# First global queries and keys by GpSimd's casting DMA, first memsets on VectorE, in an attention and feed-forward kernel

## The chip, the cores and the metric

The kernel runs on one core of a Trainium2 chip. A core has TensorE (PE, matrix products), VectorE (DVE), ScalarE (ACT), GpSimd (POOL) and SyncE (SP), all running their own instruction streams and waiting for one another through semaphores. DMAs are issued from SP, ScalarE or GpSimd; only the ones issued from GpSimd change the type on the way here (float32 in memory to bfloat16 on chip). The metric is the device time of one execution in microseconds (us), smaller is better.

## What is computed

For 8 batches and 8 heads there are 512 local tokens and 32 global tokens of 64 numbers each. Global queries attend to everything; a local query attends to the 32 global keys and to the local keys at most 32 positions away. The result goes, heads side by side, through two large matrix products with a gelu-like function between them.

```python
def _attn_ref(q_l, k_l, v_l, q_g, k_g, v_g):
    ...
    k_all = np.concatenate([k_g, k_l], axis=2)
    v_all = np.concatenate([v_g, v_l], axis=2)
    s_g = scale * np.matmul(q_g, k_all.transpose(0, 1, 3, 2))
    out_g = np.matmul(sm(s_g), v_all)
    s_ll = scale * np.matmul(q_l, k_l.transpose(0, 1, 3, 2))
    mask = np.abs(pos[:, None] - pos[None, :]) <= window      # window 32
    s_ll = np.where(mask, s_ll, -1000000000.0)
    s_lg = scale * np.matmul(q_l, k_g.transpose(0, 1, 3, 2))
    a_l = sm(np.concatenate([s_lg, s_ll], axis=-1))
    out_l = np.matmul(a_l, np.concatenate([v_g, v_l], axis=2))
    return np.concatenate([out_g, out_l], axis=2)

def _moe_ref(x, w_in, w_out):                                 # x: 4352 x 512
    h = x @ w_in                                              # w_in: 512 x 2048
    g = h * (1.0 / (1.0 + np.exp(-1.702 * h)))
    return g @ w_out                                          # w_out: 2048 x 512
```

## The kernel before

The work goes batch by batch, each batch in two quads of four heads (a quad's four heads lie in the four groups of 32 partitions). The program writes the order of every engine's instructions out by hand; the framework only adds the waits. While batch i goes through the two large products (`h_mm`, L711, and `o_mm`, L739), the attention of batch i + 1 is woven in between, so that TensorE always has work. Only the first batch has nothing to hide behind: its loads, casts, transposes and exponentials are the head of the program.

In the head, quad 0 (object `a`) and quad 1 (object `c`) of batch 0 are prepared. Keys and queries of quad 0 come as float32, in two halves each, into the tile `early`: k by ScalarE's DMA queue (L146), q by SP's (L147). ScalarE casts k's first half and then both halves of q (`cast_act`, L774); VectorE casts k's second half (L783). VectorE then transposes blocks of 32 x 32: k into `kT` (`Tk`, L335) and q into the tile `q` (`Tq`, L339), each in halves. The global queries and keys of the first two quads come by `load_g32` (L134) into float32 tiles, `g32q` ahead of q's halves on SP's queue and `g32k` behind k's halves on ScalarE's; VectorE casts them to bfloat16 (`cast_g32`, L137), transposes them (`transpose_g`, L269), and copies the global queries into the borders of the tile `q` (`ext`, L349).

TensorE begins with small products of a zero tile (L190), adds the mask's bias to the scores (`B`, L361), then three filler products of zeros (`zero`, L771), then the scores (`S`, L382), in two parts for quad 0: the first needs q's first half, the second q's second half. ScalarE takes the exponentials (`X`, L415 and L410), and so on through both quads up to L481 and L499, after which the first large product (L711) starts.

GpSimd's stream starts with memsets (`ones32` L154, `rvg` L155, `bd` L157 and L160, a border of `v` L165), the step pattern (`affine_select`, L166) from which VectorE builds `ident`, `band` and `bias` (L213 to L215), and the memset of `near_mask` (L176, read by GpSimd's `mask_near` and only needed by batch 1). Then it issues DMAs that cast: q and k of quad 1 (L78, L79), the global values `rvg` (L122, L123), and by `load_rest` v (L275), the weights w_in (L287) and w_out (L279), and batch 1. From its ninth DMA on, GpSimd issues a DMA only when its eighth-last has landed: the trace shows w_in's second load waiting for rk's landing and its eighth for v's.

The order of VectorE's instructions in the head, as the program writes it:

```python
    cast_g32("q", rqg)
    transpose_g(0, 2, "q")
    a.ext((0, 1))
    a.Tk(0, 8)
    nc.vector.tensor_copy(rk[:, 0, halves[1]], k32[:, halves[1]])
    a.Tk(8, 16)
    a.Tq(0, 8)
    a.Tq(8, 16)
    a.ext((2, 3))
    cast_g32("k", rkg)
    transpose_g(0, 2, "k")
    ...
    c.Tq()
    c.ext()
    c.Tk()
```

Of the kernel before, what the change touches and what calls it, by code (L numbers as in the profile page):

```python
# [12 lines left out]
F32 = mybir.dt.float32  # L13
# [7 lines left out]
def kernel(  # L21
# [12 lines left out]
    nc = tc.nc  # L34

    B, H, Sl, D = q_l.shape
# [18 lines left out]
    consts = ctx.enter_context(tc.tile_pool(name="consts", bufs=1))  # L55
# [8 lines left out]
    qf = q_l.rearrange("b (u j) (r t) d -> b (j r) u (t d)", j=4, t=16)  # L64
    kf = k_l.rearrange("b (u j) (r t) d -> b (j r) u (t d)", j=4, t=16)
    qgf = q_g.rearrange("b (u j) s d -> (j s) (b u) d", j=4)
    kgf = k_g.rearrange("b (u j) s d -> (j s) (b u) d", j=4)
# [4 lines left out]
    def load(b, us=(0, 1), kq=True):  # L72
        if b not in loaded:
            loaded[b] = (ld.tile([128, 2, 16 * D], BF16, name="rk"),
                         ld.tile([128, 2, 16 * D], BF16, name="rq"))
        if kq:
            s = slice(us[0], us[-1] + 1)
            nc.gpsimd.dma_start(out=loaded[b][1][:, s], in_=qf[b][:, s])  # L78
            nc.gpsimd.dma_start(out=loaded[b][0][:, s], in_=kf[b][:, s])  # L79
# [3 lines left out]
    def v_view(b, n):  # L83
        return vtiles[b % 2][:, : 8 * n * (D + 2)].rearrange("p (u j c d) -> p u j c d", u=2, j=4, c=n)
# [31 lines left out]
    rqg = consts.tile([128, NQ, D], BF16)  # L116
    rkg = consts.tile([128, NQ, D], BF16)

    rvg = consts.tile([128, 2, D + 2], BF16)

    def load_turned(eng, out_, in_):
        eng.dma_start(out=out_[32:128], in_=in_[0:96])  # L122
        eng.dma_start(out=out_[0:32], in_=in_[96:128])  # L123

    def load_g(lo, hi, names="kq"):
        for name, dst, src in (("k", rkg, kgf), ("q", rqg, qgf)):
            if name in names:
                nc.gpsimd.dma_start(out=dst[:, lo:hi, :], in_=src[:, lo:hi, :])

    g32 = {}  # L130

    def load_g32(name, src, eng):
        t = g32[name] = consts.tile([128, 2, D], F32, name="g32%s" % name)
        eng.dma_start(out=t, in_=src[:, 0:2, :])  # L134

    def cast_g32(name, t):
        nc.vector.tensor_copy(t[:, 0:2, :D], g32[name])  # L137

    load(0, kq=False)
    rk, rq = loaded[0]  # L140
    early = ld.tile([128, 4, TB], F32, name="early", bufs=1)
    k32, q32 = (early[:, 2 * i : 2 * i + 2].rearrange("p a b -> p (a b)") for i in range(2))
    halves = (slice(0, 8 * D), slice(8 * D, 16 * D))
    load_g32("q", qgf, nc.sync)
    for f in halves:
        nc.scalar.dma_start(out=k32[:, f], in_=kf[0][:, 0, f])  # L146
        nc.sync.dma_start(out=q32[:, f], in_=qf[0][:, 0, f])  # L147
    load_g32("k", kgf, nc.scalar)


    step = consts.tile([128, 289], BF16)
    nc.vector.memset(step, 1.0)
    ones32 = consts.tile([128, 32], BF16)
    nc.gpsimd.memset(ones32, 1.0)  # L154
    nc.gpsimd.memset(rvg[:, :, D:], 1.0)  # L155
    bd = consts.tile([128, 4, 32], BF16)
    nc.gpsimd.memset(bd, 0.0)  # L157
    for j in range(4):
        r = (j + 1) % 4
        nc.gpsimd.memset(bd[32 * r : 32 * r + 32, j, :], 1.0)  # L160
    vturn = [consts.tile([128, n, 8, D + 2], BF16, name="vt%d" % n) for n in (5, 4)]
    for i in range(2):
        vtiles.append(consts.tile([128, 8 * 6 * (D + 2)], BF16, name="v%d" % i))
        if i == 0:
            nc.gpsimd.memset(v_view(i, 4)[:, :, :, :, D:], 1.0)  # L165
    nc.gpsimd.affine_select(  # L166
        out=step, in_=step, pattern=[[1, 289]], compare_op=ALU.is_ge,
        fill=0.0, base=-97, channel_multiplier=-1,
    )
    tick = consts.tile([1, 2], F32)  # L170

    def after(x):
        nc.gpsimd.tensor_copy(tick[:, 0:1], x[0:1, 0:1])  # L173

    near_mask = consts.tile([128, 27, 32], BF16)
    nc.gpsimd.memset(near_mask, 1.0)  # L176
    load(0, (1,))
    load_turned(nc.gpsimd, rvg[:, 0:2, :D], vgf[:, 0:2])

    w_in_sb = wts.tile([128, 4, NKC, d_ff // 4], BF16)  # L180
# [4 lines left out]
    warm = consts.tile([128, 512], BF16)  # L185
# [63 lines left out]
    def mask_near():  # L249
        def zero(lo, hi, first, last, by):  # L250
            nc.gpsimd.memset(near_mask[lo:hi, first:last:by], 0.0)

        zero(0, 96, 4, 24, 5)
        zero(0, 96, 24, 27, 1)
        for g, first, late in ((1, 0, True), (0, 1, False), (2, 1, True), (1, 2, False), (2, 3, False), (0, 4, True)):
            mask_put(g, first, 24, 5, late, near_mask)
        zero(64, 96, 0, 24, 5)
        zero(0, 32, 2, 24, 5)
        zero(0, 64, 3, 24, 5)
        mask_put(3, 24, 25, 1, True, near_mask)  # L260

    qgT = consts.tile([128, 2, 40], F32)
    nc.vector.memset(qgT[:, :, 32:], 0.0)
    kgT = consts.tile([128, 2, 32], F32)
    def transpose_g(lo, hi, names="qk"):
        for name, dst, s in (("q", qgT, rqg), ("k", kgT, rkg)):
            if name not in names:
                continue
            nc.vector.transpose(dst[:, lo:hi, :32], s[:, lo:hi].bitcast(F32))  # L269

    def load_v2(b):
        vp = v_l[b].rearrange("(u h) (c p) d -> u p h c d", u=2, p=128)
        for u in range(2):
            for p in (slice(0, 64), slice(64, 128)):
                nc.gpsimd.dma_start(out=v_view(b, 4)[p, u, :, :, :D], in_=vp[u, p])  # L275

    def load_rest():
        def w_out(g):
            nc.gpsimd.dma_start(  # L279
                out=w_out_sb[:, 4 * g : 4 * g + 4, :].rearrange("p (g e) m -> p g (e m)", e=2),  # L280
                in_=w_out_r[:, 2 * g : 2 * g + 2, :])

        load_v2(0)
        n = d_ff // 4
        for part in range(4):
            for u in range(2):
                nc.gpsimd.dma_start(out=w_in_sb[:, part, 2 * u : 2 * u + 2],  # L287
                                    in_=w_in_r[u][:, :, part * n : part * n + n])
        w_out(1)
        load(1, (0,))  # L290
        mask_near()
        load_g(2, 4)
        load(1, (1,))
        w_out(0)
        w_out(2)
        load_v(1)
        w_out(3)
# [4 lines left out]
    def pbank(name):  # L302
        return psP.tile([128, 512], F32, name=name, tag="p")
# [440 lines left out]
    def o_out(i, tci, op):  # L744
        ob = moe.tile([128, d_model], F32, name="ob", bufs=6)
        last = i == B and tci == B // 4 - 1
        for lo, hi in ((0, 320), (320, 512)) if last else ((0, 512),):
            if last:
                op = pbank("op")
                for fc in range(FC):  # L750
                    nc.tensor.matmul(op[:, lo:hi], lhsT=gTs[i][:, fc, tci * 128 : tci * 128 + 128],  # L751
                                     rhs=w_out_sb[:, fc, lo:hi], start=(fc == 0), stop=(fc == FC - 1))
            nc.scalar.activation(ob[:, lo:hi], op[:, lo:hi], AF.Copy, scale=0.5 if i > 1 else 1.0)  # L753
            if i == B:
                rows = out.rearrange("(b s) m -> s b m", s=S)[16 * tci : 16 * tci + 16]
                nc.sync.dma_start(out=rows[:, :, lo:hi], in_=ob[:, lo:hi])
                continue
            for j in range(4):
                if 1 <= i < B:
                    r = i * S + Sg + 128 * tci + 64 * (j // 2)  # L760
                    rows = out[r : r + 64, :].rearrange("(b g q) m -> g q b m", b=2, g=2)[j % 2]
                else:
                    rows = out[i * S + Sg : (i + 1) * S, :].rearrange("(r t) m -> t r m", t=16)[4 * tci + j]
                eng = nc.gpsimd if (i, tci, j) == (B - 2, 3, 3) else nc.sync
                eng.dma_start(out=rows[..., lo:hi], in_=ob[32 * j : 32 * j + 32, lo:hi])  # L765

    a, c = Quad(0), Quad(1)

    def zero(n, ps):
        for _ in range(n):  # L770
            nc.tensor.matmul(ps, lhsT=warm[:, 0:128], rhs=warm, start=False, stop=False, skip_group_check=True)  # L771

    def cast_act(r, f32, hf):
        nc.scalar.activation(r[:, 0, halves[hf]], f32[:, halves[hf]], AF.Copy)  # L774

    cast_act(rk, k32, 0)
    cast_act(rq, q32, 0)
    cast_act(rq, q32, 1)
    cast_g32("q", rqg)
    transpose_g(0, 2, "q")  # L780
    a.ext((0, 1))
    a.Tk(0, 8)
# [2 lines left out]
    a.Tq(0, 8)  # L785
    a.Tq(8, 16)
    a.ext((2, 3))
    cast_g32("k", rkg)
    transpose_g(0, 2, "k")
    load_rest()  # L790
    a.B(0)
    a.B(1, split=True)
    zero(3, a.bk[1][3])
    a.S(0, added=True, part=0)
    a.S(0, added=True, part=1, fill=8)
    a.X(0)
# [3 lines left out]
    c.Tq()  # L800
    c.ext()
    c.Tk()
    c.B(0)
    a.K()
    a.XK()
# [40 lines left out]
    a, c = nq[1]  # L846
# [43 lines left out]
    a, c = nq[2]  # L890
# [162 lines left out]
    for st in range(4):  # L1053
        o_mm(B, st)
    o_out(B, 1, None)


# [28 lines left out]
```

## Time and profile before

| | us |
|---|---|
| median of 3 runs | 293.13 (292.99 to 293.31) |
| the profiled execution | 293.34 |
| its span, first to last instruction | 291.6 |
| PE busy in the span | 285.1 (98%) |
| DVE, ACT, POOL busy | 190.7, 163.7, 81.4 |
| granted TensorE clock, mean | 1.000 |

The profile is one execution, taken by the hardware's profiler. A row of its timeline has the start, the duration, engine and line, the operation, the tile written and the tile read, their shapes, a count, and in brackets how long the engine had stood idle before it and what ended that. An engine's name with a q (SPq) is its issuing of DMAs. The chain of work is followed back from the last instruction: each row is what the next one waited for, with start, duration and line. In the DMA view, q10 is ScalarE's queue, q1 SP's and q0 GpSimd's; a row has packets, MB, and the time of the packets as a share of 16 engines' time in the window (packets overlap, so it can exceed 100%).

### The profile page before, as it was taken

The page shows a single profiled execution, that of the slowest core. Times are in us where ns is not written, and L with a number is a line of the kernel's source. Part 1 is how long each engine was busy: PE and PEld are TensorE (multiplying, and loading weights), DVE is VectorE, ACT ScalarE, POOL GpSimd, SP SyncE. Part 2 cuts the span into 40 slices and gives each one's busy share as a digit, 9 for nine tenths or more (in the row PEclk, how much of TensorE's full clock was granted, in tenths as well). Part 3 has the DMA queues.
Part 4 walks back from the last instruction along what each step waited for, and adds up shares of the span by engine and source line. Part 5 has one row for each costly group of instructions (what it writes and reads, how often), then busy time and mean ns, then how long its engine had stood idle before and what let it go on. Part 6 is the DMA issues. An engine that isn't in the chain of part 4 may idle for free.

```text
span 291.6 us, 9957 instructions
## 1 busy us (share of the span) xinstructions
PE 285.1 (98%) x4321; PEld 145.0 (50%) x4321; DVE 190.7 (65%) x388; ACT 163.7 (56%) x272; POOL 81.4 (28%) x149
## 2 busy tenths in 40 slices
PE   7899999999999999999999999999999999999994
PEld 6454445444554455445544455445544544456553
DVE  5581856444799878787778767877777554773310
ACT  4847855665557644674556563674556541763421
POOL 8877675752155000460007000530000000000000
PEclk9999999999999999999999999999999999999999
DMA  7999993999779913899269913993272022101123
GB/s 200 175 201 207 203 144 28 193 258 205 117 120 219 190 38 70 201 197 83 58 170 179 115 42 72 219 191 46 50 191 49 2 49 65 36 0 38 37 64 84
DMA packets 56780, 35.05 MB, mean 120 GB/s; under 512 B 43312, under 2 KB 45616, under 8 KB 56736
## 3 DMA queue, kind: packets, MB, share of 16 engines
q0 software_dynamic: 47168, 17.08, 51.5%
q1 hardware_dynamic: 9008, 16.75, 22.0%
q8 instruction: 34, 0.56, 0.8%
q10 hardware_dynamic: 560, 0.59, 0.6%
q14 instruction: 10, 0.08, 0.1%
HBM read 35.19 MB, written 8.91 MB: 151 GB/s over the span
## 4 chain that ended last, share of the span: by engine, by line
PE 94%; ACT 2%; DMA 2%; SPq 0%; DVE 0%; issue 0%
PE op L739 41%; PE hp L711 38%; PE s L588 5%; PE ov L622 4%; PE s L711 2%; DMA early<-in_q_l_dram 2%; PE op L751 1%; ACT ebuf L415 1%; PE s L664 1%; PE ov L481 1%; ACT ebuf L410 1%; PE s L622 0%; PE s L382 0%; PE ov L458 0%; ACT rq L774 0%; ACT ek L446 0%
## 5 line engine op out<-in xcount | busy, mean ns | idle before, releaser
L739 PE MATMUL op<-w_out_sb,gT 128*128 128x512 bf16 x528 | 124.1, 380 | 0.0
L711 PE MATMUL hp<-xL,w_in_sb 128*128 128x512 bf16 x480 | 104.9, 379 | 0.0
L722 DVE SCALAR_TENSOR_TENSOR gT<-th,hp 128x512 bf16<-128x512 f32 (+1 forms) x112 | 71.5, 649 | 29.7 <-ACT th L721 29.1
L711 PEld LDWEIGHTS <-w_in_sb 128*128 128x128 bf16 x576 | 56.1, 98 | 64.3
L721 ACT ACTIVATE th<-hp 128x512 f32<-128x512 f32 (+1 forms) x112 | 62.7, 566 | 36.1 <-PE hp L711 35.8
L739 PEld LDWEIGHTS <-gT 128*128 128x128 bf16 x528 | 48.2, 98 | 51.2
L598 ACT ACTIVATE ebuf<-s 128x704 bf16<-128x704 f32 x48 | 33.7, 754 | 27.3 <-PE s L588 27.3
L753 ACT ACTIVATE ob<-op 128x512 f32<-128x512 f32 (+2 forms) x35 | 20.5, 585 | 42.2 <-PE op L739 35.9
L604 DVE TENSOR_TENSOR ebuf<-ebuf,mask 128x1024 bf16<-128x1024 bf16 (+1 forms) x24 | 17.4, 723 | 19.7 <-ACT ebuf L598 19.7
L99 POOL DMA_DIRECT2D v<-in_v_l_dram x35 | 27.3, 795 | 5.8 <-DMA rk<-in_k_l_dram 3.7
L553 DVE STREAM_TRANSPOSE kl<-rk 128x512 f32<-128x512 f32 x14 | 14.7, 1050 | 18.0 <-DMA rk<-in_k_l_dram 18.0
L636 DVE TENSOR_TENSOR xn<-ov,rc 128x384 bf16<-128x384 f32 (+1 forms) x39 | 21.1, 542 | 1.3
L173 POOL CAST tick<-gT 1x1 f32<-1x1 bf16 x3 | 0.5, 173 | 70.6 <-DVE gT L722 70.6
L718 ACT ACTIVATE gT<-hp 128x512 bf16<-128x512 f32 x24 | 14.3, 598 | 5.6 <-PE hp L711 5.5
L588 PEld LDWEIGHTS <-kT 32*128 32x128 bf16 x1344 | 12.4, 92 | 10.2 <-issue 9.8
L765 POOL DMA_DIRECT2D out_dram<-ob x1 | 0.5, 521 | 54.7 <-ACT ob L753 54.7
L622 PEld LDWEIGHTS <-ebuf 128*32 128x32 bf16 (+1 forms) x1312 | 12.5, 94 | 6.0 <-issue 3.0
L588 PE MATMUL s<-q,kT 32*128 32x32 bf16 (+2 forms) x1344 | 15.2, 184 | 0.0
L567 DVE STREAM_TRANSPOSE q<-rq 128x512 f32<-128x512 f32 x14 | 14.7, 1046 | 0.0
L622 PE MATMUL ov<-v,ebuf 128*32 128x66 bf16 (+1 forms) x656 | 12.4, 196 | 0.0
L635 DVE RECIPROCAL rc<-ov 128x6 f32<-128x6 f32 (+1 forms) x39 | 7.1, 183 | 7.0 <-PE ov L622 6.7
L622 PE MATMUL ov<-vt,ebuf 128*32 128x66 bf16 x528 | 10.6, 195 | 0.0
(119 smaller groups left out, 208.6 us busy)
## 6 DMA issues: line engine op xcount, KB each, us to landing
out_dram<-ob SPq DMA_DIRECT2D x127, 64.0 KB, 2.7
v<-in_v_l_dram POOLq DMA_DIRECT2D x35, 96.0 KB, 8.2
vt<-v SPq DMA_DIRECT2D x12, 264.0 KB, 4.9
vt<-v SPq DMA_DIRECT2D x6, 495.0 KB, 4.7
w_in_sb<-in_moe_w_in_dram POOLq DMA_DIRECT2D x8, 256.0 KB, 7.8
w_out_sb<-in_moe_w_out_dram POOLq DMA_DIRECT2D x4, 512.0 KB, 10.1
rq<-in_q_l_dram POOLq DMA_DIRECT2D x4, 512.0 KB, 5.9
rk<-in_k_l_dram POOLq DMA_DIRECT2D x4, 512.0 KB, 8.6
```

The lines of the kernel that those rows point to most:

```text
L99: nc.gpsimd.dma_start(out=vt[0:96, c, :, :D], in_=vs[96 * c : 96 * c + 96])
L553: nc.vector.transpose(self.kl.rearrange("p (r t) -> p t r", t=16), loaded[self.b][0][:, self.u].bitcast(F32))
L588: nc.tensor.matmul(bank(self.ps, j)[:, 0:LW].rearrange("p (t q) -> p t q", q=32)[:, os], lhsT=self.k[p, k0 : k0 + 128, e], rhs=self.q[p, t ...
L598: nc.scalar.activation(self.E[rnd][:, 2 * i : 2 * i + 2, :], self.ps[i][:, :, :LW], AF.Exp, scale=scale)
L604: nc.vector.tensor_mul(e, e, m.to_broadcast([128, 4, n]))
L622: nc.tensor.matmul(ov[32 * j : 32 * j + 32, 66 * to : 66 * to + 66], lhsT=self.E[rnd][0:n, j, 32 * o : 32 * o + 32], rhs=self.vs[rho][0:n, ...
L636: nc.vector.tensor_mul(xn[:, lo // 2 : hi // 2].rearrange("p a h w b -> p a b h w"), o3[:, 0:n, 0:D].rearrange("p (a b) (w h) -> p a b h w ...
L711: nc.tensor.matmul(hp[:, : width(i)], lhsT=w_in_c[:, fc // 4, kc, fc % 4 // 2, :, fc % 2], rhs=(xL[i] if i < B else xG)[:, kc, :], start=( ...
L721: nc.scalar.activation(th[:, :n], hp[:, :n], AF.Tanh, scale=0.851)
L722: nc.vector.scalar_tensor_tensor(gTs[i][:, fc, :n], in0=th[:, :n], scalar=1.0, in1=hp[:, :n], op0=ALU.add, op1=ALU.mult)
L739: nc.tensor.matmul(op, lhsT=gTs[i][:, fc, tci * 128 : tci * 128 + 128], rhs=w_out_sb[:, fc, :], start=(first and fc == 4 * f4), stop=(fc = ...
L753: nc.scalar.activation(ob[:, lo:hi], op[:, lo:hi], AF.Copy, scale=0.5 if i > 1 else 1.0)
```

## The change

The first global queries and keys are no longer loaded as float32 by SP and ScalarE and cast by VectorE. GpSimd's queue loads them with the cast, the queries as the very first DMA, the keys between the loads of quad 1's q and k. SP's and ScalarE's queues carry only the halves of q and k of quad 0. The memsets of `ones32`, `bd` and `near_mask` move from GpSimd to VectorE: the first two behind that of `qgT`, the last behind quad 1's transposes; `load_rest` moves in the program text to behind that one. The first three filler products become half as wide, and two output stores of the first batch are issued as two halves of 16 rows.

```diff
-    def load_g32(name, src, eng):
-        t = g32[name] = consts.tile([128, 2, D], F32, name="g32%s" % name)
-        eng.dma_start(out=t, in_=src[:, 0:2, :])
-    def cast_g32(name, t):
-        nc.vector.tensor_copy(t[:, 0:2, :D], g32[name])
+    load_g(0, 2, "q")
     load(0, kq=False)
...
-    load_g32("q", qgf, nc.sync)
     for f in halves:
         nc.scalar.dma_start(out=k32[:, f], in_=kf[0][:, 0, f])
         nc.sync.dma_start(out=q32[:, f], in_=qf[0][:, 0, f])
-    load_g32("k", kgf, nc.scalar)
...
     ones32 = consts.tile([128, 32], BF16)
-    nc.gpsimd.memset(ones32, 1.0)
-    nc.gpsimd.memset(rvg[:, :, D:], 1.0)
     bd = consts.tile([128, 4, 32], BF16)
-    nc.gpsimd.memset(bd, 0.0)
-    for j in range(4):
-        r = (j + 1) % 4
-        nc.gpsimd.memset(bd[32 * r : 32 * r + 32, j, :], 1.0)
...
-        if i == 0:
-            nc.gpsimd.memset(v_view(i, 4)[:, :, :, :, D:], 1.0)
     nc.gpsimd.affine_select(
         out=step, in_=step, pattern=[[1, 289]], compare_op=ALU.is_ge,
         fill=0.0, base=-97, channel_multiplier=-1,
     )
+    nc.gpsimd.memset(rvg[:, :, D:], 1.0)
+    nc.gpsimd.memset(v_view(0, 4)[:, :, :, :, D:], 1.0)
...
     near_mask = consts.tile([128, 27, 32], BF16)
-    nc.gpsimd.memset(near_mask, 1.0)
-    load(0, (1,))
+    nc.gpsimd.dma_start(out=rq[:, 1], in_=qf[0][:, 1])
+    load_g(0, 2, "k")
+    nc.gpsimd.dma_start(out=rk[:, 1], in_=kf[0][:, 1])
     load_turned(nc.gpsimd, rvg[:, 0:2, :D], vgf[:, 0:2])
...
     nc.vector.memset(qgT[:, :, 32:], 0.0)
+    nc.vector.memset(ones32, 1.0)
+    nc.vector.memset(bd, 0.0)
+    for j in range(4):
+        r = (j + 1) % 4
+        nc.vector.memset(bd[32 * r : 32 * r + 32, j, :], 1.0)
...
+                if i == 0 and tci == 0 and j < 2:
+                    for r in (0, 16):
+                        eng.dma_start(out=rows[r : r + 16], in_=ob[32 * j + r : 32 * j + r + 16])
+                    continue
                 eng.dma_start(out=rows[..., lo:hi], in_=ob[32 * j : 32 * j + 32, lo:hi])
...
-    def zero(n, ps):
+    def zero(n, ps, w=512):
         for _ in range(n):
-            nc.tensor.matmul(ps, lhsT=warm[:, 0:128], rhs=warm, start=False, stop=False, skip_group_check=True)
+            nc.tensor.matmul(ps[:, :w], lhsT=warm[:, 0:128], rhs=warm[:, :w], start=False, stop=False,
+                             skip_group_check=True)
...
-    cast_g32("q", rqg)
     transpose_g(0, 2, "q")
...
-    cast_g32("k", rkg)
     transpose_g(0, 2, "k")
-    load_rest()
     a.B(0)
     a.B(1, split=True)
-    zero(3, a.bk[1][3])
+    zero(3, a.bk[1][3], 256)
...
     c.Tk()
+    nc.vector.memset(near_mask, 1.0)
+    load_rest()
     c.B(0)
```

`load_g(0, 2, "q")` (L125 to L128) issues one DMA from GpSimd's queue that loads the global queries of the first two quads with the cast.

More of the change, by code (lines that the diff above doesn't have):

```diff
@@ L128, in load_g @@
                 nc.gpsimd.dma_start(out=dst[:, lo:hi, :], in_=src[:, lo:hi, :])
-    g32 = {}
-    def load_g32(name, src, eng):
-        t = g32[name] = consts.tile([128, 2, D], F32, name="g32%s" % name)
-        eng.dma_start(out=t, in_=src[:, 0:2, :])
-    def cast_g32(name, t):
-        nc.vector.tensor_copy(t[:, 0:2, :D], g32[name])
+    load_g(0, 2, "q")
     load(0, kq=False)
```

## The prediction

> **What bounds the kernel now.** The granted clock is 1.00 in every window, so all times compare directly. I read the page's part 4, the chain that ended last, first:
>
> ```profile
> PE 94%; ACT 2%; DMA 2%; SPq 0%; DVE 0%; issue 0%
> ```
>
> The kernel is one long TensorE chain with a head that is not TensorE's. The windows view says where the head ends: from 14.00 to 288.60 us PE is busy 273.73 of 274.60 us, from 0 to 14 only 11.38 of 14. After 14 us there is 0.87 us to win in all. The same chain in order of time, first 30 us (start, us, what):
>
> ```profile
> 1.33 0.45 SPq L147
> 1.78 0.04 issue
> 1.82 4.96 DMA early<-in_q_l_dram
> 6.78 0.02 issue
> 6.81 0.64 ACT rq L774
> 7.45 0.02 issue
> 7.47 0.46 DVE q L339
> 7.92 0.04 issue
> 7.97 0.48 PE s L382 x16
> 8.45 1.64 ACT ebuf L415 x2
> 10.08 1.71 ACT ebuf L410 x4
> ```
>
> So the head hangs on the landing of the second half of q (6.78), then on its cast, its transpose, the score matmuls, and from 8.45 to 13.84 on ScalarE's exponentials without a gap. Whatever the first exponential gains, the end gains, until something else is late. VectorE's timeline shows the next candidate:
>
> ```profile
> 4.21 0.23 DVE L137 CAST rqg<-g32q 128x128 bf16<-128x128 f32 x1 [0.99 <-DMA g32q<-in_q_g_dram]
> 4.47 0.25 DVE L269 STREAM_TRANSPOSE qgT<-rqg 128x64 f32<-128x64 f32 x1
> ...
> 4.94 0.60 DVE L335 STREAM_TRANSPOSE kT<-rk 128x256 f32<-128x256 f32 x1
> 5.41 0.40 DVE L783 CAST rk<-early 128x512 bf16<-128x512 f32 x1
> ...
> 7.47 0.45 DVE L339 STREAM_TRANSPOSE q<-rq 128x256 f32<-128x256 f32 x1 [0.77 <-ACT rq L774]
> ```
>
> Behind the transpose of the global queries (4.47) stand, in order, two copies, half of k's transpose, the cast of k's second half, k's other half (5.84), q's first half (6.31, ends 6.70), and only then the transpose at 7.47 that the chain waits for. VectorE's own minimum is thus 2.28 us from the 4.47 instruction to the point at which it could start the last one (6.75), and 1.34 us from the cast of k's second half. It idled 0.77 us there.
>
> **The change, part by part.** Let T be the start of the last q transpose, now 7.47.
>
> *SP.* The load of the global queries goes. It held SP from 0.81 to 1.33, so both halves of q are issued 0.52 us earlier. Its 64 KB also leave the ring ahead of q. On ScalarE's queue the 64 KB behind k's halves go; ScalarE's table load (2.23 to 3.51) can start 0.5 us earlier, which the cast of k at 4.01 does not need.
>
> *Supply of k and q.* The DMA view in half-microsecond windows gives the bytes. From 2.0 to 3.5 ScalarE's queue, nearly alone, moves 0.32 MB and SP's 0.06. With both at work, 3.5 to 4.0:
>
> ```profile
> q10 hardware_dynamic: 68, 0.13, 65.7%
> q1 hardware_dynamic: 98, 0.08, 49.6%
> ```
>
> That is 0.20 MB in half a microsecond; 3.5 to 5.5 gives 0.69 MB, or 0.17 per half. k and q are 1.05 MB. With 0.10 MB by 2.5 as now and 0.17 per half from there, the last byte is moved at 2.5 + 0.95/0.17 x 0.5 = 5.3 us; at 0.20 it is 4.9, at 0.15 it is 5.7. Landing follows by some 0.3 us on the slower engines: the last landing of k and that of q at about 5.6 each (bounds 5.0 and 6.2). For q that is 1.2 us earlier. For k it is later: its bytes are now through by 5.0, as it has the engines to itself first. k's first half shares too: 0.52 MB of both are moved at about 3.8 instead of 0.26 MB at 3.3, so ScalarE's first cast goes from 4.01 to about 4.3 (4.0 to 4.5), and the three casts of 0.63 us follow as 4.3, 4.95 and 5.65, the last ending at 6.3.
>
> By the Trainium skill, page "DMA: Bandwidth & Descriptors", section "Issuing engines are not separate DMA queues", loads of all queues share 16 engines, and spreading them saves issue time alone: that would be the 0.52 us of SP and no more. The row agrees in part: with both queues busy the engines' shares add to 115%, but one queue alone left them at 69%.
>
> *Global queries on GpSimd's queue.* Everything there starts at 0.80. The same transfer later in the kernel (L128, rqg) holds GpSimd 0.73 us. First bytes: the first load on this queue now, rq, is issued at 3.02 and the queue's first 3 packets fall in 5.0 to 5.5, so 2.0 to 2.5 us on; for an issue at 0.80 that is 2.8 to 3.3. Then 256 small packets beside k and q. Lower bound for landing: 0.3 us of transfer, 3.6. Upper: rq's whole 5.1 us from issue to landing, for eight times the bytes, 5.9. Between: g32q took 3.4 us on SP's queue beside one busy queue, and 0.5 more for the later first bytes gives 4.7. I take 4.6. Its cast (0.23 plus 0.03) is gone, so the transpose can start at 4.6 where it is now 4.47: T no earlier than 4.6 + 2.28 = 6.9.
>
> *T.* From k's second half: 5.6 + 0.02 + 1.34 = 6.95. From q's cast: 6.3. From the globals: 6.9. T is 6.95 against 7.47, a gain of **0.5 us**. Bounds: with k at 5.0, globals at 4.0 and ScalarE's first cast at 4.0, that cast decides: k's first transpose at 4.65 instead of 4.94 and T 1.81 behind it, 6.46 (gain 1.0); with k at 6.2, T is 7.55 (loss 0.1); with globals at 5.9, T is 8.2 (loss 0.7).
>
> *GpSimd up to the loads of v.* Removed: ones32 and bd (0.12 + 0.20 + 0.59) and near_mask (0.81). Added: two issues (0.73 and 0.77, the L128 rows). New order from 0.80: 0.73 + 0.42 + 0.10 + 0.14 + 0.70 + 0.77 + 0.55 + 0.66 + 0.54 ends at 5.41; now v's loads start at 5.44. So v, w_in and what follows are unmoved; they have cover anyway (v is landed before 15, first used at 15.11; kl at L553 gets its rk at 29.26 and its matmuls start at 33.6, over 1 us after the operands). rq of the second quad is issued at 2.2 instead of 3.02, rk at 3.7 as now, the global keys before rk. The global keys stand behind 256 KB and land near 7.8, about when VectorE reaches them (7.5 to 8.0), and their cast (0.22) goes. VectorE then is some 0.3 us ahead at the second quad's transposes, which end at 10.66 where TensorE needs them at 11.25 less the gain.
>
> *VectorE.* ones32, bd and its four blocks are six memsets of 0.07 to 0.17 (rows: 0.07 for 16 elements, 0.17 for 128), about 0.55 us, in the 0.99 us of idle time before 4.21; step's mask comes 0.36 us earlier too. Without that cover they would cost 0.55 on T. near_mask, 864 elements at step's 0.30 us per 289, is 0.90 us from 10.66 on; it has 0.74 us of idle and pushes eg from 11.40 to 11.56, which TensorE reads at 15.86. Nothing.
>
> *TensorE and the output.* The three filler matmuls (1.09 us, ending 6.63 just before q's first half is ready at 6.70) are halved; that keeps them out of the way of an earlier start and gains nothing alone. Two more output issues on SP cost 0.5 us each there, off the chain.
>
> **Sum.** The profiled execution took 293.34 (span 291.6 and 1.7 around it); less 0.5 it is 292.8. The median of the runs, 293.13, is 0.2 below the profiled one: **292.6**.
>
> **Rivals.**
> 1. *Late globals (slower).* Their small packets queue beside two full queues, and T hangs on them. It decides from a landing at 5.2 on (5.2 + 2.28 = 7.47). If each engine serves one small packet per k and q packet, 16 of them wait until k and q are through: landing about 5.5 to 5.9, with a late first byte 6.2. Price 0.3 to 1.0: 293.4 to 294.1. For: two full queues, where g32q had one beside it. Against: from 53.0 to 53.5 us GpSimd's queue moves 466 packets while SP's moves 25, so small packets are not held to one for one. The Trainium skill, same page, section "Queues, rings and completion order", has engines take turns by packets of some 9 to 17 descriptors; by that these globals need one or two turns and land near 4.1, and this rival falls.
> 2. *Crowding (no change).* k's second half, with SP's queue and, from about 4.6, the earlier rq beside it, lands at 5.9 to 6.2: T is 7.25 to 7.55, time 292.9 to 293.2. For: rq's queue, once it ran, left SP's queue 0.09 MB in 1.5 us (5.5 to 7.0). Against: most of k is moved before rq's bytes start.
> 3. *The gain is absorbed.* If rk of the second quad lands later than its 9.6, its transposes end past 10.7 and c's scores start no earlier. Price: the gain, 293.1. Against: its queue starts earlier.
>
> **Numbers.** Forecast (gain 0.3 to 1.0) 0.61, late globals 0.20, crowding 0.15, absorbed 0.04. A measurement of this kernel can tell about 0.2%, 0.59 us, from no change; the forecast sits just under that edge. Faster takes gains of 0.59 to 1.0, six tenths of the forecast's range, 0.38; slower by as much is the worse end of the first rival, 0.15; the rest, 0.47, is within. The range holds the forecast, crowding and most of the first rival: 292.0 to 293.9. The forecast's own is 292.1 to 292.8.
>
> **What would show it.** Right: the chain's DMA piece ends near 5.6 and may name k instead of q; the transpose of the global queries near 4.6; last q transpose near 6.95, first exponential near 7.9; everything from 14 us on shifted by the same half microsecond. Wrong: VectorE waits for rqg past 5.2; or the first exponential gains and TensorE at 33 us does not.

## The result and the profile after

The changed kernel takes **295.36 us** (median of 6 runs, 295.17 to 296.13) against 293.34 for the kernel before in the same comparison (6 runs, 292.99 to 293.80): ratio 1.0063, interval 1.0036 to 1.0090. It is slower by 2.0 us, where 0.5 us faster was forecast; the time lies above the range. The profiled execution took 295.17 with a span of 293.4, against 293.34 and 291.6, and its mean granted clock is 0.993 instead of 1.000.

Part 4 of the page, the changed kernel; it answers to the line with 94% for PE:

```profile
PE 93%; issue 2%; DMA 2%; ACT 1%; DVE 1%; POOLq 0%
```

The DMA piece is still 2%, but another one. The chain of waits of the changed kernel, first 16 us (start, us, what):

```profile
1.33 5.16 DMA rqg<-in_q_g_dram
6.49 0.02 issue
6.51 0.26 DVE qgT L258
6.77 0.02 issue
6.79 0.28 DVE q L338 x2
7.07 0.52 DVE kT L324
7.59 0.27 DVE rk L776
7.85 0.02 issue
7.88 0.61 DVE kT L324
8.48 0.27 DVE q L328
8.75 0.04 issue
8.79 0.43 PE s L371 x16
...
10.83 1.06 PE s L764 x2
11.89 1.12 PE s L350 x8
13.01 0.59 PE kb L390 x8
13.60 0.02 issue
13.62 0.60 ACT ek L435
14.22 1.64 ACT ebuf L404 x2
```

The head now hangs on the global queries, which land at 6.49 us; before it hung on q's second half at 6.78. VectorE's six steps behind them take from 6.51 to 8.79, so the first scores start 2.28 us behind the transpose. In the lower rows TensorE is slow: two fillers of 512 columns take 1.06 us, where the kernel e3 below has 0.59 for the same two, and 8 bias matmuls take 1.12. The windows of the changed kernel show why (columns: window, its length in us, busy time in us and count of PE, PEld, VectorE, ScalarE and GpSimd, granted clock, DMA share, GB/s):

```profile
9.00:10.00 1.00, 1.00 (x56) 0.89 (x44) 1.00 (x7) 0.36 (x1) 1.00 (x2) 0.71 2.29 154
10.00:11.00 1.00, 0.67 (x17) 0.41 (x11) 1.00 (x5) 1.00 (x2) 0.98 (x3) 0.50 2.42 154
11.00:12.00 1.00, 1.00 (x5) 0.47 (x4) 0.89 (x2) 1.00 (x4) 1.00 (x2) 0.50 2.45 169
12.00:13.00 1.00, 1.00 (x12) 0.73 (x13) 0.38 (x2) 1.00 (x3) 1.00 (x3) 0.59 1.82 173
13.00:14.00 1.00, 1.00 (x25) 0.39 (x24) 0.00 (x0) 0.38 (x2) 1.00 (x2) 1.00 1.26 181
```

From 9.4 to 12.8 us TensorE runs at half its clock; before it had 1.00 there. ScalarE, full from 10 to 13 us, is then empty for 0.62 of 1.00 us, as `ek` waits for TensorE's `kb`.

**Where the 2 us come from.** Four landmarks of the two traces: the first exponential moves from 8.43 to 9.64 (+1.21); quad 1's first in the chain from 12.28 to 14.22 (+1.94); the activation tables loaded at 16.89, 33.25 and 53.11 by +2.02, +2.03 and +2.03; the last activation from 287.90 to 289.95 (+2.05). So 1.21 us come from the late globals, 0.81 from 8.4 to 16.9 us, where the clock is low, and nothing from the other 270 us.

### The profile page after: what moved, and what is told of

Same layout as the page of the kernel before. It is cut to its first block, busy times and chain, and to the rows that moved or that the text cites. A ratio compares the mean times of both kernels' runs of the same rounds, so it can differ in the third digit from the quotient of the medians.

```text
span 293.4 us, 9903 instructions
## 1 busy us (share of the span) xinstructions
PE 280.5 (96%) x4266; PEld 145.6 (50%) x4321; DVE 191.2 (65%) x393; ACT 163.7 (56%) x272; POOL 81.8 (28%) x144
## 4 chain that ended last, share of the span: by engine, by line
PE 93%; issue 2%; DMA 2%; ACT 1%; DVE 1%; POOLq 0%
PE op L728 39%; PE hp L700 38%; PE s L577 5%; PE ov L611 4%; PE s L700 2%; DMA rqg<-in_q_g_dram 2%; PE op L740 1%; PE s L653 1%; PE s L371 1%; PE ov L470 1%; ACT ebuf L404 1%; PE s L350 1%; PE s L611 0%; DVE kT L324 0%; PE s L764 0%
## 5 line engine op out<-in xcount | busy, mean ns | idle before, releaser
L728 PE MATMUL op<-w_out_sb,gT 128*128 128x512 bf16 x483 | 118.4, 380 | 4.0 <-issue 2.5
```

What stands on the lines that cost most here:

```text
L728: nc.tensor.matmul(op, lhsT=gTs[i][:, fc, tci * 128 : tci * 128 + 128], rhs=w_out_sb[:, fc, :], start=(first and fc == 4 * f4), stop=(fc = ...
```

## The experiments

In this table the first columns are shifts in us against the profiled execution of the kernel before at four of these landmarks; "idle" is the largest wait of TensorE just ahead of the score matmuls of quad 0, "clock" the lowest granted clock in the windows of 1 us from 9 to 13. The last columns are the medians and ratios to the kernel before on the same chip (its median is 293.02 to 293.34 throughout). The landmarks are those of one execution of each kernel, and kernels with the same head differ in them by some 0.1 to 0.3 us (the first exponential is at 9.64, 9.59 and 9.47 in the changed kernel, e3 and e11). Mechanisms are read from the landmarks, and the medians carry the verdicts.

| kernel | first exp | 16.89 | 53.11 | last act. | idle | clock | median | ratio, 95% |
|---|---|---|---|---|---|---|---|---|
| changed | +1.21 | +2.02 | +2.03 | +2.05 | 2.36 | 0.50 | 295.36 | 1.0063 [1.0036, 1.0090] |
| e1 globals' route undone | +2.19 | +2.97 | +2.98 | +2.82 | 2.48 | 0.50 | 297.32 | 1.0144 [1.0076, 1.0211] |
| e2 only globals' route changed | +0.91 | +0.91 | +1.91 | +1.85 | 0.37 | 1.00 | 295.25 | 1.0061 [1.0037, 1.0085] |
| e3 changed, long filler | +1.16 | +1.16 | +1.17 | +1.66 | 0.91 | 1.00 | 295.83 | 1.0083 [1.0052, 1.0114] |
| e4 globals alone first | – | +9.29 | +9.29 | +10.84 | 9.24 | 0.50 | 304.10 | one run |
| e5 globals between k's halves | +0.71 | +0.71 | +0.72 | +0.74 | 1.28 | 1.00 | 294.64 | 1.0042 [1.0015, 1.0069] |
| e6 one memset off GpSimd | +1.30 | +2.25 | +2.26 | +2.12 | 1.85 | 0.50 | 295.04 | 1.0049 [1.0012, 1.0087] |
| e7 one more memset on GpSimd | −0.43 | −0.43 | +0.51 | +0.41 | 0.72 | 1.00 | 293.88 | 1.0016 [0.9994, 1.0039] |
| e8 only global keys on GpSimd | −0.74 | −0.56 | −0.02 | −0.19 | 0.36 | 1.00 | 293.58 | 1.0017 [0.9991, 1.0043] |
| e9 e8 and k ahead of q | −0.47 | −0.31 | −0.30 | −0.41 | none | 1.00 | 293.10 | 0.9992 [0.9973, 1.0012] |
| e10 k ahead of q | −0.14 | −0.14 | −0.13 | −0.26 | 0.52 | 1.00 | 293.20 | 0.9987 [0.9964, 1.0011] |
| e11 changed, first filler as before | +1.04 | +1.89 | +1.90 | +3.45 | 1.93 | 0.50 | 295.06 | 1.0050 [1.0018, 1.0082] |
| e12 changed, k and q later | +1.90 | +2.75 | +2.76 | +3.51 | 2.76 | 0.50 | 296.73 | one run |

The kernel before has an idle time of 0.67 by the same measure and clock 1.00.

### Is it the globals' route? e1 and e2

**e1** is the changed kernel with the globals loaded as float32 by SP and ScalarE and cast by VectorE again; the moved memsets and the short filler stay.

```diff
-    load_g(0, 2, "q")
+    load_g32("q", qgf, nc.sync)          # and "k" on nc.scalar, with both casts
...
-    load_g(0, 2, "k")
```

> The changed kernel with only the route of the globals undone (float32 by SP and ScalarE, cast on VectorE); the moved memsets, the halved filler and the split stores stay. Theory A (globals land 1.3 us too late and the TensorE gap that follows drops the clock): both go, first exponential at 8.2 to 8.6 us, clock 1.00 throughout, time that of the kernel before within 0.4 us. Theory B (the halved filler drops the clock by itself): first exponential near 8.4, but clock 0.5 in some stretch between 9 and 13 and 0.7 us more than before. Theory D (the memsets on VectorE and GpSimd's new order cost it): about as slow as the changed kernel, 1.5 to 2 us above before.

It got slower still, by 2.8 us at the last activation and by 4.2 in the median of its four runs. The chain of waits of e1, first 10 us:

```profile
1.82 7.12 DMA early<-in_q_l_dram
8.95 0.02 issue
8.97 0.64 ACT rq L777
9.61 0.02 issue
9.63 0.46 DVE q L337
```

q's second half, issued at 1.82 as in the kernel before, takes 7.12 us instead of 4.96. Nothing ahead of it changed on its queue; what changed is that GpSimd, rid of its memsets, issues its first casting load at 1.82 instead of 3.02. No expectation had this way for the loss.

**e2** is the kernel before with the globals' route alone changed.

```diff
-    load_g32("q", qgf, nc.sync)
+    load_g(0, 2, "q")
...
+    load_g(0, 2, "k")                    # between quad 1's q and k
```

> The kernel before with only the route of the globals changed to GpSimd's casting queue; memsets stay on GpSimd, filler full width. A: the global queries land at 6.2 to 6.8, first exponential at 9.4 to 9.8; the clock falls if the 0.55 us of wider filler is too little, time 1.2 us above before with the clock up and 1.9 with it down. B: clock 1.00 all the way, 1.2 above before. D: within 0.4 us of before.

The route alone costs 0.91 us in the head: `rqg` is issued at 1.33 and lands 4.9 us later. The clock holds; the step pattern comes late behind the load, the fillers end late, and TensorE idles only 0.37 us. Another 1.0 us goes between 33 and 53 us: `kl` of batch 1 waits for k until 32.45 instead of 29.26, and the scores at 35.54 wait for it. So the 2 us of e2 and the 2 us of the change are two different sums.

### Why do the globals land late? e4 and e12

**e4** is the changed kernel with the DMAs of k and q held until the globals have landed (four copies from `rqg` into `early` ahead of them).

```diff
+    for i in range(4):
+        nc.vector.tensor_copy(early[:, i, 0:1], rqg[:, 0, 0:1])
     for f in halves:                     # k and q issued here
```

> The changed kernel with the four loads of k and q held back until the global queries have landed, so that their load meets idle DMA engines (the time is several us longer for that and is not of interest). Starved: the queue's first packets come 2.0 to 2.5 us after the issue and it lands within 3.5 us of it, against 3.7 and 5.2 in the changed kernel. First use: the first load of GpSimd's queue needs 3.5 us or more to its first packet whatever else runs.

**e12** holds them only to 2.12 us, by four memsets of `early` behind other VectorE work, so that they overlap with the globals on the way.

```diff
+    for i in range(4):
+        nc.vector.memset(early[:, i, 0:1], 0.0)
     for f in halves:                     # k and q issued here
```

> The changed kernel with the four loads of k and q held until about 2.2 us, 1.4 us later than now, by memsets on VectorE that write their first columns; the global queries are issued at 1.33 as now. If the queue that has its packets up first goes first, the global queries land at 3.7 to 4.3 (2.4 to 3.0 us after their issue) though k and q are the same amount and in flight by 3.6. If the two hardware queues hold GpSimd's back whenever they are busy, the queries land near 7. The first exponential is at 9.3 to 10.2 either way, as k's first half lands at 6 to 6.5.

In both, one execution each, the globals are issued at 1.33 as in the changed kernel. From issue to landing, in the changed kernel and in e12 (e4 has the same line):

```profile
DMA to landing us min/median/max: 5.2/5.2/5.2
```

```profile
DMA to landing us min/median/max: 2.4/2.4/2.4
```

Thus no cost of a first use, and no length of the transfer itself. Nor is it the memsets on VectorE: e4 and e12 have them and land early, e2 does not have them and needs 4.9 us. The DMA view tells who moves bytes. The changed kernel, from 4.5 to 5.0 us and then from 5.0 to 5.5 (queue, packets, MB, share of 16 engines):

```profile
q1 hardware_dynamic: 62, 0.12, 63.2%
q10 hardware_dynamic: 41, 0.08, 41.2%
```

```profile
q10 hardware_dynamic: 72, 0.13, 66.4%
q0 software_dynamic: 86, 0.01, 34.3%
q1 hardware_dynamic: 24, 0.03, 14.9%
```

Up to 5.0 us GpSimd's queue, issued at 1.33, moves nothing; its first packets come at about 5.3, as SP's queue runs dry. In e4, with no other packets about, they begin at about 2.9. In e12 its globals pass ahead of k and q, but its next load, issued at 2.77, has 1 packet up to 6.5 us and 16 from 6.5 to 7.0, beside 48 and 30 of the hardware queues. (k's first half is cast from 6.79 on there and the first exponential comes at 10.33, both a little later than expected.) In the kernel before, whose first load on GpSimd's queue is issued at 3.02, the window from 5.0 to 5.5 has:

```profile
q0 software_dynamic: 3, 0.01, 8.8%
```

An earlier issue does not bring GpSimd's bytes forward at all: in the twelve kernels whose k and q are issued at their usual time (all but e4 and e12) its first packets fall between 5.0 and 5.7 us, whether the first load is issued at 1.33, 1.82, 2.27, 3.02 or 3.90. By 5.25 us the changed kernel has moved 0.94 of the 1.05 MB of k and q. Whether GpSimd's packets were ready and not served, or were themselves made late, no run here shows. The Trainium skill, page "DMA: Bandwidth & Descriptors", section "Queues, rings and completion order", has each engine take turns between queues by packets; for GpSimd's queue these windows show no turn from 2.9, where e4 has its first packet, to 5.0 us, which agrees with that only if its packets were not there yet.

It works the other way round as well. e1's 7.12 us and, in e4, 8.0 to 9.9 us from issue to landing for the halves of k and q are hardware-queue transfers held up beside GpSimd's loads, in e4 behind loads already running. e6 takes that alone.

### One memset, forward and back: e6 and e7

**e6** is the kernel before with only the memset of `near_mask` (0.8 us) moved from GpSimd to VectorE. `load_rest` moves behind it in the program text, which leaves the order of GpSimd's loads as it was.

```diff
-    nc.gpsimd.memset(near_mask, 1.0)
...
-    load_rest()
...
     c.Tk()
+    nc.vector.memset(near_mask, 1.0)
+    load_rest()
```

> The kernel before with one edit: the 0.8 us memset of near_mask goes from GpSimd to VectorE, so GpSimd's casting loads are issued 0.8 us earlier. Theory S (the deeper GpSimd's queue is when k's and q's tail is moved, the longer the last q packets wait): q's second half lands at 7.3 us or later instead of 6.78, first exponential and end 0.5 to 2.2 us later. Rival R (the late landing in the run with only the globals' route undone came from something else): as before within 0.2 us.

GpSimd's loads are issued 0.75 us earlier, from 2.27 on, and the kernel loses 2.1 us at the last activation (1.75 in the median). The chain of waits of e6:

```profile
1.82 6.27 DMA early<-in_q_l_dram
8.09 0.02 issue
8.12 0.64 ACT rq L773
```

And its DMA view from 6.75 to 8.75 us:

```profile
q0 software_dynamic: 206, 0.38, 105.7%
q1 hardware_dynamic: 4, 0.01, 1.0%
q10 hardware_dynamic: 8, 0.00, 0.5%
```

The last four packets of q, all that SP's queue still has, come singly among GpSimd's 206: one by 7.1 us, two to 7.6, one behind that. The memset was no idle work: it kept the issue of GpSimd's loads late enough for q to pass. GpSimd's first packet comes between 5.2 and 5.3 us in both kernels, so it is not its start that hurts q; why an earlier issue leaves q's last packets behind, no run shows.

**e7** is the kernel before with that memset made twice on GpSimd, so that the first load is issued at 3.90.

> The kernel before with a second, useless memset of near_mask on GpSimd, so that its casting loads are issued 0.8 us later. S: q's second half lands at 6.0 to 6.5, the first exponential comes 0.2 to 0.5 us earlier; the end gains that, unless quad 1's k (9.6 before, then about 10.2) is late for its scores, then within 0.2 us of before. R: q's second half at 6.8 as before, end 0 to 0.3 us later.

q lands 0.43 us earlier, and the head gains that. It does not last: batch 1's loads are now later, `kl` starts at 31.05 instead of 29.26, and the scores behind it wait 0.79 us. Instead of −0.43 the end has +0.41, which the timing (1.0016, interval down to 0.9994) cannot tell from no change.

### What the supply of k allows: e5

**e5** is the kernel before with the global queries (float32) on ScalarE's queue between k's halves, and q alone on SP's; GpSimd is untouched.

```diff
-    load_g32("q", qgf, nc.sync)
     for f in halves:
         ...
+        if f is halves[0]:
+            load_g32("q", qgf, nc.scalar)
```

> The kernel before with the float32 load of the global queries moved from the head of SP's queue to between k's two halves on ScalarE's queue, so that q's halves are issued 0.5 us earlier, the globals are early enough, and GpSimd is untouched. If the prediction's supply step was right (k's first half at 4.3, k's and q's last halves at 5.6), the first exponential comes 0.3 to 0.6 us earlier than before. If both queues starting together starve k's first half (4.6 to 5.1 in the three runs with that start), nothing is gained: first exponential within 0.3 us of 8.43 and the time within 0.3 us of before, or worse.

With both queues starting together, k's first half lands at 4.97 instead of 4.0 and the globals at 5.58, and the head loses 0.71. The loss is that of the globals, for which VectorE waits 2.38 us; what bears on the supply is k's landing. In the changed kernel, too, k's first half is cast from 5.11 on, not from 4.01, and from 4.80 and 4.67 in e3 and e11, whose loads are the same. From 2.0 to 3.5 us the two queues of the changed kernel move 0.15 and 0.12 MB, 0.27 together (0.30 and 0.31 in e3 and e11); in the kernel before ScalarE's queue, nearly alone, moved 0.32 of 0.38 MB. So there was little gain to be had even with the globals in time: ScalarE's first cast plus 0.65 and the 1.81 us behind it, both from the prediction, put the last q transpose at 7.57, 7.26 and 7.13 in these three, against 7.47 in the kernel before. That is a gain of 0.3 us at the most, and in the changed kernel's own execution none.

### What the low clock costs: e3 and e11

**e3** is the changed kernel with 14 short fillers instead of 3, so that TensorE works until 7.86 us.

```diff
-    zero(3, a.bk[1][3], 256)
+    zero(14, a.bk[1][3], 256)
```

> The changed kernel with 14 fillers of 256 columns instead of 3 ahead of the first scores, so that TensorE's idle time from 6.4 to 8.8 is mostly filled. A: first exponential stays at 9.6 to 9.8, clock 1.00 all the way, and the time drops by 0.6 to 0.8 us to some 1.2 above before. If the low clock had cost nothing, the time stays within 0.2 of the changed kernel.

The timeline of e3 (in brackets the idle time ahead):

```profile
8.77 0.43 PE L371 MATMUL s<-q,kT 32*128 32x120 bf16 x16 [0.91 <-DVE q L328]
```

The same row of the changed kernel:

```profile
8.79 0.43 PE L371 MATMUL s<-q,kT 32*128 32x120 bf16 x16 [2.36 <-DVE q L328]
```

The scores start at the same time, but the clock stays at 1.00 (e3, same columns as above), and the shift stays at 1.16 to 53 us instead of growing to 2.03.

```profile
10.00:11.00 1.00, 0.84 (x16) 0.57 (x14) 1.00 (x5) 1.00 (x2) 1.00 (x2) 1.00 2.43 155
```

That shows the 0.86 us as the clock's. e3's median does not confirm it: its runs scatter from 294.59 to 297.87, with a mean granted clock of 0.998 or more in all of them, its interval overlaps that of the changed kernel, and its own profiled execution loses another 0.5 us after 75 us, for a cause that stays open. As a change to make, e3 is unproven.

**e11** gives the changed kernel its three fillers of 512 back.

```diff
-    zero(3, a.bk[1][3], 256)
+    zero(3, a.bk[1][3])
```

> The changed kernel with only the first three fillers back at 512 columns. They run 0.5 us longer, so TensorE's idle time ahead of the first scores falls from 2.36 to about 1.85 us, which is what it was in the run with near_mask's memset moved, where the clock fell to 0.5. If the idle time decides, the clock falls here too and the time stays within 0.3 us of the changed kernel's; if the halving was the cause of the low clock, it is 1.00 throughout and the time 0.6 to 0.9 us lower. The first exponential stays at 9.6 either way.

TensorE still idles, and the clock falls as before. Timeline of e11:

```profile
8.64 0.43 PE L371 MATMUL s<-q,kT 32*128 32x120 bf16 x16 [1.93 <-DVE q L328]
```

Halving the fillers is therefore not needed for the low clock; with full fillers a wait of 1.93 us brought it, and without the wait (e3) it did not come. e11's profiled execution loses a further 1.5 us late, which its median of 295.06 does not.

Across the table the extra shift from the first exponential to 16.89 us sorts by idle time. With up to 1.28 us it is 0 (0.18 and 0.16 in e8 and e9, at clock 1.00, where TensorE waits 0.34 and 0.31 for `eg`); with 1.85, 1.93, 2.36, 2.48 and 2.76 it is 0.95, 0.85, 0.81, 0.78 and 0.85, and the clock is at 0.50. Worked out from the windows' granted clock, the drop comes 0.2 to 0.9 us after the scores have begun and 2.6 to 3.5 us behind the start of the wait, and the half clock lasts 3.4 us in all five. The Trainium skill, page "TensorE: Matmul & The Clock Gate", section "Part 1: The HAM clock gate (the "warmup" mystery)", gives the half clock after an idle window of about 3.4 us that runs free; here an idle time of 1.85 us was enough, though the delay is of that size. The traces have a reading in which whole waits are not needed: in the 3.41 us just ahead of the drop TensorE was busy 0.71 to 1.56 us in the five, and in the kernels without a drop no stretch of that length that starts from 4.5 to 9.9 us has less than 1.97 (e5). No run here varies that busy time apart from the wait, and one profile of each kernel does not fix the threshold.

The other executions bear on it too, as each has its mean granted clock on record. One stretch of 3.4 us at half clock makes 0.994 of a mean of 1.000 over 293 us. All six runs of the changed kernel are at 0.994 or below, seven of e11's ten, eight of e6's ten, and five of e5's ten, so that the same program does both. Within one kernel the runs at 0.994 or below are the longer ones: medians of 295.18 against 294.50 in e11, 295.23 against 294.62 in e6, 294.73 against 294.07 in e5. That agrees with the price, at 0.6 to 0.7 us, in runs of one and the same program. It does not isolate it, as a run with a longer wait would have both, and in the kernel before the few runs at 0.994 or below are longer by over 2 us.

### What caps a gain in the head: e8, e9 and e10

**e8** is the kernel before with only the global keys on GpSimd's queue, between quad 1's q and k; the global queries stay on SP's.

```diff
-    load_g32("k", kgf, nc.scalar)
...
+    load_g(0, 2, "k")
```

> The kernel before with only the global keys moved, from the tail of ScalarE's queue to GpSimd's casting queue between quad 1's q and k. 256 small packets less beside q's second half: S and the prediction's step on supply both have q's second half at 6.3 to 6.7 and the end 0.1 to 0.4 us earlier. If q's tail only depends on GpSimd's queue, no change (within 0.1).

The head gains 0.74 us. ScalarE's queue has 64 KB less, and GpSimd's large loads have one more issue in between; which of the two does it was not tried apart. By 53 us it is gone. Timeline of e8, VectorE and then TensorE:

```profile
30.50 1.05 DVE L554 STREAM_TRANSPOSE kl<-rk 128x512 f32<-128x512 f32 x1 [7.85 <-DMA rk<-in_k_l_dram]
...
33.60 0.66 PE L665 MATMUL s<-q,kT 32*128 32x160 bf16 x32 [0.39 <-DVE kT L577]
```

In the kernel before `kl` starts at 29.26 and these scores at 33.61 without a wait. They start at the same time in both: batch 1's k has become the limit.

**e9** adds to e8 that k is issued ahead of q from batch 1 on; **e10** has that alone.

```diff
-            nc.gpsimd.dma_start(out=loaded[b][1][:, s], in_=qf[b][:, s])
             nc.gpsimd.dma_start(out=loaded[b][0][:, s], in_=kf[b][:, s])
+            nc.gpsimd.dma_start(out=loaded[b][1][:, s], in_=qf[b][:, s])
```

> The kernel before with the global keys on GpSimd's queue (as in the run with that one edit, where the first exponential came 0.74 us earlier and all was given back between 33 and 48 us) and, from batch 1 on, each batch's k loaded ahead of its q instead of behind it. If the gain was lost because VectorE waits for batch 1's k (30.5 us) and nothing else, k now lands 1 us earlier, the lead of about 0.55 us at 33 us holds to the end, and the time is 0.5 to 0.8 us below before. If the whole load stream bounds that stretch, the lead is lost again and the time is within 0.2 us of before.

> The kernel before with only k ahead of q in the loads from batch 1 on. In the kernel before VectorE has batch 1's operands ready 1 us before TensorE wants them, so an earlier k gains nothing: within 0.2 us of before.

With k first, `kl` starts at 29.36, the scores at 33.30 do not wait, and e9's lead of 0.31 us at 16.89 is 0.30 at 53 and 0.41 at the last activation. The 0.5 to 0.8 us that were expected of e9 did not come: the lead was kept, but it began with 0.47 at the first exponential, where e8, with the same head, had 0.74. e10's `kl` starts at 28.60, with a lead of 0.13. Both medians are the lowest of the study (293.10 and 293.20, against 293.33 in that comparison), but the intervals take in 1: a gain of this size is below what the timing can tell.

## Why the prediction was wrong

- **What bounds the kernel: right.** The head decides, and what it loses the end loses: +2.02 at 16.89 us, +2.05 at the last activation.
- **VectorE's chain: right, to 0.13 us.** Behind the globals' transpose T was to come 2.28 us later. The two q transposes of 0.40 us now fill 0.72 us from 8.34 on, so the last starts at 8.66, 2.15 behind 6.51. T is 8.66 where 6.95 was forecast and 7.47 was before, and the first exponential follows 0.98 later, as before (0.96).
- **The globals' landing: the step that failed.** "I take 4.6"; it was 6.49, beyond even the upper bound of 5.9. GpSimd's DMA is issued at 1.33, not "at 0.80", 0.53 us of it. The rest is the first-byte time of 2.0 to 2.5 us, read from rq, which was issued at 3.02 and moved first bytes past 5.0, and carried over to the earlier issue. It could not be: the first packets come between 5.2 and 5.3 us in both kernels, though the first issue is 1.69 us earlier. With nothing ahead (e4 and e12) they come some 1.5 us after the issue, and the whole landing takes 2.4; so rq's row was in part a wait for full queues, and for an earlier issue it grows instead of staying.
- **The supply of k and q: wrong too.** ScalarE's first cast was put at 4.3 (4.0 to 4.5); it starts at 5.11, and at 4.80 and 4.67 in e3 and e11 with the same loads. e5 (4.97) shows the same without a new load on GpSimd. By this step alone at most 0.3 us of the forecast 0.5 was within reach. The last bytes of k and q, put at 5.3, were moved before 6.0 us.
- **GpSimd up to v: right in its sum, wrong in its worth.** v's first load is issued at 5.79, where 5.41 was forecast, by the late start. But its memsets were counted as free time, and the earlier start of rq as harmless; e1 and e6 show that the memsets, by delaying the issue of GpSimd's loads, let q through, which is worth 1.3 to 2.2 us of the head where the globals do not wait already.
- **Rival 1, late globals: it happened, and was priced too low.** Its landing was 5.5 to 6.2 and its price 0.3 to 1.0; the head alone lost 1.21. The argument against it, 466 packets to 25 at 53 us, was from one hardware queue with 25 packets in that window, not from two full ones. The prediction's own sign of being wrong, a wait of VectorE for rqg past 5.2, came.
- **The clock: missed.** "The granted clock is 1.00 in every window, so all times compare directly" was taken over to the changed kernel. A wait of 2.36 us on TensorE cost some 0.8 us more behind it (e3), and no rival had this. Nor does the 1.00 of the view fit the first 6 us of the kernel before, by the durations in its own trace: the bias products (L361) take 340 to 368 ns there from 4.8 to 6 us and 229 to 247 from 9 to 13, and 314 to 368 in the half-clock stretch of the changed kernel (L350).
- **Rival 2, crowding:** it did not come to a test. VectorE reaches k's second half at 7.45, without a wait for it.
- **Rival 3, absorption:** not in the change, where there was no gain to absorb, but e7 and e8 show it, at batch 1's k at 33 us and not at quad 1's rk.
- **VectorE's memsets, `near_mask` and the two output issues:** hidden, as put. The small memsets lie before 4.2 us, ahead of a wait of 2.31 us; from 16.89 us to the end the shift changes by 0.03.

## What to carry to other kernels

A time to the first byte that is read while other queues are full contains a wait for them, and is not a latency to carry to an earlier issue: ask whose packets are under way first. Work that stands ahead of a DMA issue can protect another transfer, so taking it away is a change in the order of transfers and is to be priced as one. And a forecast that adds a wait on TensorE of some 2 us should add what the clock takes afterwards, and a forecast of a gain should look for the next load that comes just in time.

## What the runs showed of the hardware

- GpSimd's casting queue and the hardware queues hold each other up: the globals took 2.4 us with nothing ahead and 4.9 to 5.2 behind k and q; q's second half took 4.96 with GpSimd's loads issued from 3.02 on, 6.27 and 7.12 from 2.27 and 1.82 on; and halves of k and q took 8.0 to 9.9 behind a running queue.
- Behind k and q, GpSimd's first packets came between 5.0 and 5.7 us for first issues from 1.33 to 3.90.
- Two hardware queues that started together moved less at first than one nearly alone: 0.27 to 0.31 against 0.38 MB from 2.0 to 3.5 us.
- In the profiled executions half clock for 3.4 us followed idle times of 1.85 us and more, and none followed up to 1.28 us; by the mean clock of the other runs, e5 and e11 do both.
- As the program's first instruction on GpSimd a DMA started at 1.33 us, where a memset started at 0.80.
